# Attention, Fourier mixing and an MLP on one core: the same steps in another written order

## The chip, the cores and the metric

The kernel runs on one core of a Trainium2 chip. A core has five engines with an instruction queue each: TensorE (PE, matrix products), VectorE (DVE), ScalarE (ACT), GpSimd (POOL) and SyncE (SP, which here only issues DMAs). An engine runs its queue strictly in order; across engines, semaphores make an instruction wait for its inputs and for the release of a buffer. 16 DMA engines move data between HBM and the on-chip memory (SBUF); PE writes its products to a second memory (PSUM). The metric is the device time of one execution in microseconds, here the median of several runs. Lower is better.

## The reference

The inputs are q, k and v of shape 4 x 8 x 768 x 64 (batch, heads, sequence, head width) and the two weights of an MLP, 512 x 2048 and 2048 x 512, all float32.

```python
# attention over selected blocks of 64 keys
k_rep = k.reshape(B, H, n_blocks, block, D).mean(axis=3)
gate_scores = np.einsum('bhsd,bhnd->bhsn', q, k_rep)
gate_scores = np.where(causal, gate_scores, -1000000000.0)
top_idx = np.argsort(gate_scores, axis=-1)[..., -top_k:]          # top_k = 3
# mask: the selected blocks and the own block, causal inside
scores = np.where(mask, scale * np.matmul(q, k.transpose(0, 1, 3, 2)), -1000000000.0)
attn = softmax(scores); x = np.matmul(attn, v)                    # then heads side by side: 4 x 768 x 512
# Fourier mixing, normalisation, MLP
mixed = np.real(np.fft.fft(np.fft.fft(x, axis=1), axis=2))
u = x + mixed
un = (u - mean(u)) / np.sqrt(var(u) + 1e-06)
out = u + np.maximum(un @ w_ch1, 0.0) @ w_ch2
```

## The kernel before

**Tiling.** The attention works on 16 pairs of heads, P = 0 to 15; pairs 4b to 4b+3 make up batch b. When the four pairs of a batch are done, its x (768 x 512) is folded, goes through two Fourier transforms as matrix products, is normalised, and goes through the MLP. So the work of a batch is a long chain of small steps (attention, Fourier) and then a block of pure PE work (the MLP), and the attention of later pairs is interleaved with the MLP of earlier batches.

**The order.** No planner runs in the kernel. The string `ORDER` (from line 112) lists 1011 steps, each a name and its numbers. Lines 753 to 758 call the function behind each (the table `WORK`, line 735) in that order, inside `tc.manual_schedule` for all five engines. Each engine's queue is therefore the list of the steps that issue on it, in the order of the string; where two steps on different engines stand in the string relative to each other means nothing by itself. Semaphores and the choice of a free buffer are the framework's.

**The steps, by engine.**

- SP: `Lk:P`, `Lq:P`, `Lv:P` load k, q and v of a pair (line 264; k and q as two DMAs of 192 KB, v as one of 384 KB; three buffers each for k and q, two for v). `LF`, `LT`, `Lc`, `Li` load constants; `LF` and `LT` are the Fourier matrices. `un:b,i` for b of 1 and more is a pair of transposing DMAs (line 593). `od:b,i` writes a block of the result.
- POOL: `W:c` and `X:c` issue the DMAs of the MLP weights, `W:0` 512 KB, `W:1` and `W:2` 768 KB, `X:0` and `X:1` 1024 KB as fp16 in SBUF (lines 721 to 729); their targets are tiles of their own, so they wait for nothing but their turn in POOL's queue. `qs:P` and `vc:P` cast q and v, `d:P,i` clears the upper triangle of a diagonal block (line 437), `K:P` copies the mask rows, `nr:b` makes the reciprocal root, `pg:b` is a tiny copy that waits for the folded tile of batch b.
- PE: `tk:P` and `tq:P` transpose k and q (line 292), `g:P` gives the gate scores, `s:P,i` six tiles of scores (lines 409 to 421, from pair 7 on line 414), `v:P` the product with v (line 449), `y` and `m` the Fourier products, `xt` three transposes of batch 0, `w:b,i` 16 steps of the first MLP product (lines 629 and 631) and `c:b,i,h` 12 half-steps of the second (line 656; line 648 for the last block).
- DVE: `ks`, `kh`, `qc` on the transposed k and q, `gt`, `gx`, `gl`, `gm` the choice of blocks, `x:P` the softmax division, `fs`, `fd`, `f` the folds, `tr` a reversed copy, `u` the sum x + mixed, `un:0,i` copies of batch 0, `bn` and `nv` the statistics, `r:b,i` the relu of every fourth `w`, `o` the last sum.
- ACT: `kc:P` casts the transposed k, `e:P,i` the exponentials (line 431), `ty` a copy, `xu` the centred u, and the other `r`.

**Waits around the change.** `tk:P` needs `Lk:P`, `tq:P` needs `Lq:P`. `v:P` needs `vc:P`, which needs `Lv:P`, and all of `d:P,i`. `s:P,i` needs `qs:P`, `kc:P` and `gm:P` (from pair 7 on also `K:P`). `e:P,i` needs `s:P,i`. `f:b,*` and then `y:b,*` need `x` of the batch's four pairs. `w:b,i` needs all `un` of the batch. All PSUM tiles share four buffers. u has five buffers of two blocks each, which `od` releases.

Of the kernel before, what the change touches and what calls it, by code (L numbers as in the profile page):

```python
# [787 lines left out]
```

## Time and profile before

| what | us |
|---|---|
| median of 3 runs | 297.64 |
| lowest and highest of them | 297.6, 297.93 |
| profiled execution, first to last instruction | 295.6 |
| PE busy in it | 286.5 |
| DVE busy | 192.5 |
| ACT busy | 164.2 |
| POOL busy | 111.1 |

The table's last rows are the busy time of each engine inside the span. PE is busy for most of it, but the profile models the ends of matmuls, so a matmul that is held up counts as busy. A row of 40 digits gives the busy share of 40 equal slices in tenths. Queue q0 carries the weights, which POOL issues; q1 carries what SP issues. For a DMA the profile has the start of its issue and the time to its landing. In a list of stages the numbers are the length, the busy time and the count of instructions of PE, PE's weight loads, DVE, ACT and POOL, the granted clock of PE, the share of the DMA engines and GB/s.

### The profile page before, as it was taken

The page shows a single profiled execution, that of the slowest core. Times are in us where ns is not written, and L with a number is a line of the kernel's source. Part 1 is how long each engine was busy: PE and PEld are TensorE (multiplying, and loading weights), DVE is VectorE, ACT ScalarE, POOL GpSimd, SP SyncE. Part 2 cuts the span into 40 slices and gives each one's busy share as a digit, 9 for nine tenths or more (in the row PEclk, how much of TensorE's full clock was granted, in tenths as well). Part 3 has the DMA queues.
Part 4 walks back from the last instruction along what each step waited for, and adds up shares of the span by engine and source line. Part 5 has one row for each costly group of instructions (what it writes and reads, how often), then busy time and mean ns, then how long its engine had stood idle before and what let it go on. Part 6 is the DMA issues. An engine that isn't in the chain of part 4 may idle for free.

```text
span 295.6 us, 6738 instructions
## 1 busy us (share of the span) xinstructions
PE 286.5 (97%) x2633; PEld 180.2 (61%) x2633; DVE 192.5 (65%) x597; ACT 164.2 (56%) x205; POOL 111.1 (38%) x286
## 2 busy tenths in 40 slices
PE   8899999999999999999999999999999999999995
PEld 4566767765676556656757667446666554555453
DVE  2999999986988638987796577714493282700132
ACT  3698989749578841677788843165524250155000
POOL 2267528528776289064753363220303000110000
PEclk9999999999999999999999999999999999999999
DMA  8999999997999727477000005311000052300023
GB/s 197 268 228 230 262 245 199 195 230 118 226 185 211 168 55 186 118 164 176 3 0 2 0 9 136 38 72 71 2 1 2 32 103 44 142 0 2 0 91 125
DMA packets 93200, 33.53 MB, mean 113 GB/s; under 512 B 85936, under 2 KB 89968, under 8 KB 93168
## 3 DMA queue, kind: packets, MB, share of 16 engines
q1 hardware_dynamic: 87504, 28.47, 40.6%
q0 software_dynamic: 3664, 4.19, 9.1%
q10 hardware_dynamic: 2000, 0.44, 0.7%
q8 instruction: 21, 0.34, 0.5%
q14 instruction: 11, 0.09, 0.1%
HBM read 28.63 MB, written 6.29 MB: 118 GB/s over the span
## 4 chain that ended last, share of the span: by engine, by line
PE 84%; DVE 7%; ACT 6%; DMA 1%; issue 1%; DVEq 0%; ACTq 0%
PE c L656 26%; PE h L629 19%; PE h L631 10%; PE sc L414 7%; PE av L449 6%; ACT pt L431 5%; PE tp L292 5%; PE yp L519 2%; PE mx L552 2%; DVE q L316 2%; PE mx L553 1%; PE warmps L693 1%; DVE u L566 1%; PE g L342 1%; PE c L648 1%; PE sc L409 1%
## 5 line engine op out<-in xcount | busy, mean ns | idle before, releaser
L431 ACT ACTIVATE pt<-sc 128x1024 f16<-128x1024 f32 (+1 forms) x96 | 83.3, 923 | 26.6 <-PE sc L414 19.7
L629 PE MATMUL h<-unT,w 128*128 128x512 f16 x256 | 85.1, 379 | 0.0
L656 PE MATMUL c<-w_sb,hT 128*128 128x512 f16 x368 | 83.8, 379 | 0.0
L631 PE MATMUL h<-unT,w 128*128 128x256 f16 x256 | 69.7, 272 | 0.4 <-DMA unT<-x 0.4
L641 ACT ACTIVATE hT<-h 128x768 f16<-128x768 f32 x48 | 37.8, 813 | 43.7 <-PE h L631 43.7
L656 PEld LDWEIGHTS <-hT 128*128 128x128 f16 x368 | 35.6, 98 | 39.3 <-issue 0.5
L437 POOL TENSOR_SCALAR_AFFINE_SELECT pt<-pt 128x256 f16<-128x256 f16 x96 | 37.5, 414 | 58.5 <-ACT pt L431 57.6
L629 PEld LDWEIGHTS <-w 128*128 128x128 f16 x256 | 25.0, 97 | 29.2 <-issue 1.3
L668 DVE SCALAR_TENSOR_TENSOR u<-c,rs,u 128x512 f32<-128x512 f32 (+1 forms) x25 | 17.5, 725 | 31.2 <-PE c L656 30.4
L639 DVE TENSOR_SCALAR hT<-h 128x768 f16<-128x768 f32 x16 | 15.3, 955 | 29.7 <-PE h L631 29.6
L578 ACT ACTIVATE x<-u,nm 128x512 f16<-128x512 f32 x24 | 15.9, 715 | 22.5 <-DVE nm L572 22.3
L292 PE MATMUL tp<-id,nat 128*128 128x128 f32 x192 | 27.5, 284 | 0.6 <-ACT pt L431 0.3
L631 PEld LDWEIGHTS <-w 128*128 128x128 f16 x256 | 25.0, 98 | 4.3
L225 POOL TENSOR_SCALAR_AFFINE_SELECT qk<-mt 32x160 f16<-32x160 f16 x72 | 23.1, 341 | 10.8 <-DVE mt L386 9.1
L414 PE MATMUL sc<-qk 96*128 96x512 f16 (+3 forms) x144 | 26.8, 305 | 0.0
L225 POOL TENSOR_SCALAR_AFFINE_SELECT qk<-q 64x768 f16<-64x768 f32 (+1 forms) x25 | 20.6, 825 | 14.8 <-DVE q L316 14.1
L292 PEld LDWEIGHTS tp<-id,nat 128*128 128x128 f32 x192 | 22.2, 146 | 5.7 <-issue 1.6
L449 PE MATMUL av<-v,pt 128*128 128x65 f16 x672 | 23.0, 193 | 0.1
L449 PEld LDWEIGHTS <-pt 128*128 128x128 f16 x672 | 22.0, 97 | 1.7 <-POOL pt L437 0.5
L297 DVE TENSOR_REDUCE kr<-tp 128x12 f32<-128x768 f32 x16 | 15.1, 945 | 5.9 <-PE tp L292 5.9
L222 POOL TENSOR_TENSOR t<-vr,rs 128x6 f32<-128x6 f32 x12 | 2.4, 199 | 43.5 <-DVE rs L609 42.9
L414 PEld LDWEIGHTS <-qk 96*128 96x128 f16 x144 | 13.3, 97 | 8.9 <-issue 0.5
(95 smaller groups left out, 351.2 us busy)
## 6 DMA issues: line engine op xcount, KB each, us to landing
nat<-in_v_dram SPq DMA_DIRECT2D x16, 384.0 KB, 4.7
nat<-in_k_dram SPq DMA_DIRECT2D x31, 192.0 KB, 3.5
nat<-in_q_dram SPq DMA_DIRECT2D x31, 192.0 KB, 3.9
out_dram<-u SPq DMA_DIRECT2D x23, 256.0 KB, 2.1
w_sb<-in_moe_w_ch_dram POOLq DMA_DIRECT2D x2, 1024.0 KB, 10.2
w<-in_moe_w_ch_dram POOLq DMA_DIRECT2D x2, 768.0 KB, 8.4
fs_sb<-c_FS SPq DMA_DIRECT2D x1, 582.0 KB, 5.1
w<-in_moe_w_ch_dram POOLq DMA_DIRECT2D x1, 512.0 KB, 7.3
```

The source lines that it names most:

```text
L225: nc.gpsimd.affine_select(out=out, in_=in_, pattern=[[0, i] for i in n], base=0, channel_multiplier=0, compare_op=ALU.is_ge, fill=0.0)
L292: nc.tensor.transpose(ps[:, 128 * st:128 * st + 128], src[:, st, :], id32)
L414: nc.tensor.matmul(ps[:, e, co:co + q1 - q0], qk[0:96, e, 1, 128 * jt:128 * jt + 128], qk[0:96, e, 0, q0:q1], start=True, stop=True)
L431: nc.scalar.activation(out=d["pt"][:, o:o + 2 * n].rearrange("p (e c) -> p e c", e=2), in_=d["sc", i][:, :, 0:n], func=AF.Exp, scale=0.125)
L437: nc.gpsimd.affine_select(out=dg, in_=dg, pattern=[[0, 2], [1, 128]], base=0, channel_multiplier=-1, compare_op=ALU.is_ge, fill=0.0)
L449: nc.tensor.matmul(av[:, e, 66 * st:66 * st + 65], pt[:, co:co + 128], vv[:, e, jt, 0:65], start=(cnt == 0), stop=(cnt == 20))
L578: nc.scalar.activation(out=x_b[:, 2 * kp + k2, :], in_=u_b[:, k2, :], func=AF.Identity, scale=0.0625, bias=nm[:, k2:k2 + 1])
L629: nc.tensor.matmul(hp[:, 0:512], w1s, unT[:, dt, 0:512], start=(dt == 0), stop=(dt == NDT - 1))
L631: nc.tensor.matmul(hp[:, 512:768], w1s, unT[:, dt, 512:768], start=(dt == 0), stop=(dt == NDT - 1))
L641: nc.scalar.activation(out=hT, in_=hp, func=AF.Relu)
L656: nc.tensor.matmul(c_ps[b, g[0]][:, st - g[0], :], h_t[b, it][:, 128 * st:128 * (st + 1)], w2_sb[:, it, :], start=(it == 0), stop=(it == N ...
L668: nc.vector.scalar_tensor_tensor(out=o, in0=ps, scalar=st_t[b][1][:, st:st + 1], in1=o, op0=ALU.mult, op1=ALU.add)
```

## The change

Only the string `ORDER` changes. It holds the same 1011 steps, each once, in another order on all five engines. On POOL, the weight loads `W:1`, `X:1`, `X:0` and `W:2` move to the front part of the queue, `W:0` moves behind `vc:5`. On SP, among others, `Lv:2` and `Lv:3` move ahead of `Lv:1`, and `Lk:7`, `LF`, `Lk:8` and `LT` change places with other loads. On PE, DVE and ACT neighbouring steps change places in the attention part (`v:1` now stands ahead of `s:3,1`, for one), and around each MLP the mix of `c`, `w`, `s` and `v` steps is another. In the new string the steps of POOL and SP stand in bunches; the sequence on each engine is what counts.

```diff
 ORDER = """
-Lk:1 Lq:1 Lk:2 Lq:2 tk:0 ks:0 tq:0 Lq:3 Lk:3 kh:0 qc:0 iz:1 tk:1 qs:0 kc:0 g:0 ks:1 iz:0 gt:0 tq:1
-kc:1 gx:0 Lq:4 Lv:0 Lk:4 Lv:1 kh:1 gl:0,0 tk:2 gl:0,1 gm:0 kc:2 qc:1 s:0,3 s:0,2 ks:2 e:0,3 qs:1
-tq:2 Lq:5 Lk:5 s:0,5 qc:2 g:1 e:0,5 e:0,2 kh:2 s:0,4 gt:1 qs:2 s:0,0 e:0,4 gx:1 s:0,1 d:0,2 tq:3
-gl:1,0 e:0,0 gl:1,1 tk:3 gm:1 e:0,1 d:0,0 qc:3 g:2 d:0,3 kc:3 d:0,5 s:1,5 gt:2 d:0,4 s:1,0 e:1,5
-qs:3 ks:3 s:1,4 e:1,0 tq:4 d:0,1 gx:2 vc:0 e:1,4 s:1,3 qc:4 s:1,1 Lv:2 e:1,3 s:1,2 gl:2,0 kh:3
-tk:4 gl:2,1 e:1,2 d:1,3 gm:2 g:3 d:1,4 ks:4 d:1,0 v:0 d:1,5 gt:3 vc:1 kc:4 gx:3 e:1,1 s:2,5 Lv:3
-Lq:6 LF:0 Lq:7 Lk:6 Lk:7 LT:0 s:2,3 kh:4 gl:3,0 e:2,5 gl:3,1 s:2,4 e:2,3 d:1,1 x:0 tq:5 qs:4 e:2,4
-g:4 d:2,3 gm:3 qc:5 s:2,0 d:2,4 s:2,2 d:1,2 e:2,0 gt:4 d:2,5 tk:5 vc:2 gx:4 e:2,2 s:2,1 ks:5 d:2,0
-Lv:4 Lq:8 Lk:8 s:3,1 e:2,1 v:1 gl:4,0 kh:5 gl:4,1 kc:5 d:2,1 gm:4 d:2,2 s:3,2 x:1 e:3,1 vc:3 g:5
-e:3,2 Lv:5 Lc:0 d:3,1 s:3,5 gt:5 s:3,0 fs:0,1 e:3,5 s:3,3 d:3,2 gx:5 e:3,0 s:3,4 fs:1,1 tq:6
-gl:5,0 e:3,3 fs:0,0 v:2 gl:5,1 fs:1,0 e:3,4 d:3,3 qc:6 d:3,0 s:4,5 x:2 d:3,4 s:4,4 e:4,5 d:3,5
-s:4,0 qs:5 v:3 e:4,0 gm:5 fs:2,0 fs:2,1 e:4,4 s:5,5 x:3 s:4,1 e:5,5 s:5,1 e:4,1 fd:2,0 s:4,2 s:5,0
-fs:3,1 e:5,1 fs:3,0 s:5,2 fd:2,1 e:5,0 fd:3,1 s:4,3 fd:3,0 e:5,2 tk:6 f:0,1 f:0,2 e:4,3 Lk:9 Lq:9
-tk:7 f:0,3 e:4,2 f:0,0 y:0,1 ks:7 pg:0 W:0 kc:6 y:0,0 tr:0,1 d:4,0 kc:7 d:4,4 d:4,5 ks:6 d:5,5
-d:4,1 ty:0,1 tr:0,0 s:5,3 d:5,2 s:5,4 d:4,3 kh:6 W:1 ty:0,0 m:0,2 qs:6 e:5,3 u:0,2 m:0,1 vc:4
-e:5,4 m:0,0 u:0,1 xu:0,2 d:5,4 tk:8 d:5,1 d:4,2 u:0,0 xu:0,1 d:5,0 xt:0,2 W:2 g:6 un:0,2 xu:0,0
-xt:0,1 gt:6 tq:8 un:0,1 kc:8 xt:0,0 qc:8 tq:7 un:0,0 qs:8 v:4 Lq:10 Lk:10 Lv:6 Lq:11 qc:7 bn:0,3
-w:0,4 d:5,3 qs:7 bn:0,1 w:0,5 r:0,4 gx:6 ks:8 w:0,6 r:0,5 gl:6,0 kh:7 gl:6,1 x:4 w:0,7 r:0,6 gm:6
-w:0,3 r:0,7 s:6,5 r:0,3 s:6,1 e:6,5 s:6,3 e:6,1 kh:8 s:6,2 fs:4,0 bn:0,4 w:0,2 e:6,2 d:6,1 X:0
...
-vc:7 e:7,2 tq:10 gl:8,1 Lv:9 r:0,1 X:1 gm:8 s:7,4 qc:10 w:0,15 d:7,2 e:7,4 K:8 bn:0,0 g:9 r:0,15
...
-m:1,0 o:0,0 m:1,1 od:0,0 o:0,1 d:9,2 od:0,1 v:8 u:1,1 m:1,2 u:1,0 xu:1,1 c:0,4,0 gl:11,0 xu:1,0
...
-qc:13 vc:13 bn:1,4 s:11,2 d:10,5 x:9 s:11,4 vc:12 e:11,2 c:0,5,1 bn:1,1 Lv:14 Lv:15 e:11,4 s:11,0
-o:0,5 s:11,5 w:1,11 e:11,5 od:0,5 o:0,4 e:11,0 kh:12 bn:1,5 od:0,4 s:11,3 w:1,7 e:11,3 r:1,11
...
-d:14,5 x:12 qs:15 s:14,3 m:2,2 e:14,3 bn:2,0 c:1,4,0 x:13 fs:13,0 g:15 fs:13,1 c:1,5,0 u:2,2
-fs:12,0 xu:2,2 gt:15 c:1,2,0 bn:2,4 un:2,2 gx:15 c:1,5,1 gl:15,0 fs:12,1 gl:15,1 gm:15 bn:2,5
-c:1,4,1 K:15 c:1,2,1 o:1,4 od:1,4 o:1,5 s:14,1 od:1,5 s:15,4 e:14,1 s:15,0 c:1,3,0 e:15,4 d:14,1
-d:14,3 e:15,0 d:15,4 s:14,4 s:14,2 d:15,0 e:14,4 s:15,2 c:1,3,1 e:15,2 e:14,2 s:15,3 o:1,3 w:2,1
...
-c:2,1,0 r:2,12 ty:3,0 c:2,0,1 c:2,1,1 m:3,0 o:2,0 c:2,2,0 od:2,0 u:3,0 o:2,1 xu:3,0 m:3,1 od:2,1
-c:2,4,0 u:3,1 un:3,0 xu:3,1 bn:3,2 m:3,2 c:2,3,0 u:3,2 un:3,1 bn:3,3 xu:3,2 c:2,5,0 bn:3,0 un:3,2
-bn:3,5 c:2,3,1 bn:3,1 c:2,4,1 c:2,2,1 w:3,3 c:2,5,1 r:3,3 o:2,3 w:3,7 od:2,3 o:2,4 o:2,2 od:2,4
...
-r:3,12 r:3,9 r:3,14 c:3,0,0 w:3,15 c:3,4,0 r:3,15 c:3,1,0 c:3,0,1 c:3,1,1 c:3,5,0 o:3,0 od:3,0
-o:3,1 c:3,3,0 od:3,1 o:3,5 od:3,5 c:3,4,1 c:3,2,1 o:3,4 od:3,4 c:3,3,1 c:3,5,1 o:3,3 od:3,3 o:3,2
-od:3,2 o:3,6 od:3,6
+Lk:1 Lq:1 Lk:2 Lq:2 tk:0 Lk:3 Lq:3 ks:0 kc:0 tq:0 tk:1 kh:0 qc:0 g:0 tq:1 tk:2 kc:1 iz:0 iz:1 ks:1
+kc:2 gt:0 W:1 qs:0 Lq:4 Lv:0 Lk:4 Lv:2 Lq:5 Lv:3 Lk:5 Lv:1 Lk:7 Lq:6 kh:1 gx:0 gl:0,0 gl:0,1 gm:0
+s:0,3 tq:2 s:0,2 s:0,5 e:0,3 qc:1 e:0,5 g:1 e:0,2 s:0,4 e:0,4 s:0,0 e:0,0 ks:2 s:0,1 qc:2 e:0,1 tq:3
+gt:1 gx:1 gl:1,0 kh:2 gl:1,1 X:1 d:0,5 d:0,2 qs:1 gm:1 qc:3 tk:3 g:2 s:1,5 kc:3 e:1,5 s:1,0 s:1,4
+e:1,0 tq:4 gt:2 s:1,3 ks:3 s:1,1 gx:2 kh:3 s:1,2 tk:4 qc:4 g:3 e:1,4 gl:2,0 gl:2,1 gm:2 qs:2 d:0,1
+d:0,0 vc:0 d:0,4 d:0,3 X:0 d:1,5 vc:2 W:2 d:1,4 ks:4 v:0 s:2,5 s:2,3 s:2,4 gt:3 e:1,3 e:1,2 gx:3 x:0
+tq:5 kh:4 g:4 e:1,1 kc:4 e:2,5 e:2,3 e:2,4 fs:0,1 gl:3,0 s:2,0 qc:5 gl:3,1 gt:4 s:2,2 e:2,0 s:2,1
+gm:3 gx:4 fs:0,0 d:1,2 qs:3 d:1,1 qs:4 d:2,3 d:1,3 d:1,0 vc:1 tk:5 ks:5 e:2,1 v:1 gl:4,0 kh:5 x:1
+kc:5 s:3,1 e:2,2 e:3,1 s:3,2 e:3,2 g:5 gl:4,1 fs:1,0 s:3,5 e:3,5 s:3,4 s:3,0 s:3,3 e:3,4 tq:6 e:3,0
+gt:5 e:3,3 LF:0 Lk:8 LT:0 Lv:5 Lv:4 Lk:6 Lv:6 Lq:11 Lk:10 Lv:7 Lk:12 Lq:8 Lq:7 Lv:8 Lk:9 Lq:9 Lc:0
+d:2,2 d:2,5 d:2,4 d:3,1 vc:3 d:2,0 d:3,5 d:2,1 d:3,2 d:3,0 d:3,3 d:3,4 qs:5 gm:4 gx:5 gl:5,0 fs:1,1
+gl:5,1 qc:6 v:2 s:4,5 e:4,5 s:4,0 s:4,4 v:3 gm:5 s:5,5 e:4,0 s:4,1 e:4,4 e:5,5 x:2 e:4,1 s:5,0 e:5,0
+s:5,2 e:5,2 s:4,2 s:5,1 s:4,3 tk:7 e:4,2 fs:2,0 fs:2,1 fd:2,1 x:3 fd:2,0 fs:3,0 fs:3,1 fd:3,0 fd:3,1
+f:0,2 f:0,3 f:0,0 f:0,1 y:0,1 tr:0,1 e:4,3 e:5,1 ks:7 ty:0,1 y:0,0 tr:0,0 s:5,3 kc:7 tk:6 m:0,2 ks:6
+s:5,4 ty:0,0 kc:6 e:5,3 m:0,1 kh:6 u:0,2 e:5,4 m:0,0 g:6 u:0,1 u:0,0 xu:0,2 xu:0,1 vc:5 W:0 d:5,5
+d:4,1 qs:6 vc:4 d:5,2 pg:0 d:5,3 d:4,0 d:4,5 d:5,4 d:4,3 d:5,1 vc:6 d:4,2 d:5,0 d:4,4 xu:0,0 xt:0,2
+tk:8 gt:6 un:0,2 xt:0,1 un:0,1 tq:8 xt:0,0 un:0,0 kc:8 gx:6 qc:8 v:4 w:0,4 w:0,6 w:0,5 tq:7 ks:8
...
+bn:1,3 u:1,0 s:10,1 xu:1,0 e:10,1 m:1,2 u:1,2 c:0,5,0 xu:1,2 od:0,1 od:0,2 od:0,3 un:1,0 un:1,1
+un:1,2 tq:13 v:9 qc:13 e:11,5 s:10,2 e:10,2 c:0,5,1 s:10,5 s:10,4 e:10,5 tq:12 s:11,2 s:11,4 e:10,4
+tk:13 tk:12 w:1,6 x:9 o:0,4 w:1,14 e:11,4 w:1,11 e:11,2 w:1,7 kc:12 o:0,5 kc:13 fs:8,1 qc:12 s:11,3
...
+c:1,2,0 g:15 o:1,1 c:1,3,0 s:14,0 m:2,2 gt:15 c:1,5,1 gx:15 gl:15,0 gl:15,1 gm:15 d:14,2 K:15 s:15,0
+e:14,0 xu:2,0 s:15,5 u:2,2 c:1,3,1 o:1,5 s:14,5 e:15,5 e:15,0 xu:2,2 s:15,3 e:15,3 s:15,4 o:1,4
+o:1,3 bn:2,4 c:1,2,1 e:15,4 s:15,1 s:15,2 e:14,5 od:1,0 Lv:14 od:1,1 un:2,1 un:2,0 un:2,2 s:14,1
+w:2,13 e:15,1 w:2,5 w:2,4 e:15,2 e:14,1 r:2,5 r:2,4 o:1,2 bn:2,5 bn:2,2 nv:2 d:15,3 d:14,0 d:15,5
...
+r:2,9 w:2,15 r:2,10 r:2,15 ty:3,0 c:2,0,1 o:2,0 y:3,1 c:2,1,1 ty:3,1 tr:3,0 m:3,0 c:2,2,1 tr:3,1
+m:3,1 c:2,4,0 o:2,1 m:3,2 u:3,0 c:2,4,1 c:2,5,0 u:3,1 u:3,2 bn:3,2 c:2,3,1 c:2,5,1 od:1,3 od:1,4
+od:1,2 od:2,0 od:2,1 od:1,5 xu:3,0 xu:3,1 xu:3,2 un:3,0 un:3,1 un:3,2 bn:3,3 w:3,11 bn:3,0 o:2,5
...
+c:3,3,0 c:3,3,1 c:3,0,1 o:3,3 o:3,4 c:3,1,0 o:3,0 c:3,1,1 c:3,2,1 o:3,1 o:3,2 c:3,5,1 od:3,5 od:2,5
+od:3,3 od:2,4 od:2,3 od:2,2 od:3,4 od:3,1 od:3,0 od:3,2 o:3,6 od:3,6
 """
```

## The prediction

> **What bounds the kernel now.** I read the page first, then sums by stage, the chain of waits, the DMA issues in order of time, and the landing times of single loads. Columns are named where they are not plain.
>
> The page: busy time by engine, then the span in 40 slices of 7.4 us, then two DMA queues with packets, MB and share of the span.
>
> ```profile
> PE 286.5 (97%) x2633; PEld 180.2 (61%) x2633; DVE 192.5 (65%) x597; ACT 164.2 (56%) x205; POOL 111.1 (38%) x286
> ...
> DMA  8999999997999727477000005311000052300023
> ...
> q1 hardware_dynamic: 87504, 28.47, 40.6%
> q0 software_dynamic: 3664, 4.19, 9.1%
> ```
>
> PE looks full, but the 97% hides a start that is not. The stages (length, then busy us of each engine, clock, DMA share, GB/s) show it:
>
> ```profile
> 0.00:20.00 20.00, 17.24 (x151) 10.87 (x152) 14.03 (x51) 12.28 (x16) 7.13 (x28) 1.00 1.01 227
> 20.00:32.00 12.00, 11.56 (x214) 8.30 (x214) 11.36 (x51) 10.48 (x13) 7.94 (x17) 1.00 1.08 249
> 32.00:58.60 26.60, 24.51 (x388) 19.07 (x385) 25.38 (x70) 24.43 (x31) 13.59 (x28) 1.00 1.06 220
> 58.60:292.20 233.60, 233.16 (x1890) 141.93 (x1886) 141.31 (x429) 117.06 (x146) 82.40 (x217) 1.00 0.37 84
> ```
>
> From 58.6 us, where the first `w:0,4` (line 629) starts, PE idles 0.44 us in 233.6. Before that ACT and DVE are nearly full while PE's matmuls are stretched. And in the first three stages the DMA engines are at a share of 1.01 to 1.08: full. The chain of waits (start, us) agrees: ACT and DVE carry it until the first batch's `un` copies, PE after that.
>
> ```profile
> 32.02 1.95 ACT pt L431 x2
> ...
> 39.94 5.89 ACT pt L431 x7
> ...
> 54.52 0.60 DVE unT L590
> ...
> 58.76 0.22 PE h L629
> ```
>
> How far ahead of their use do the q, k and v loads run? In the order of time, SP's and POOL's issues:
>
> ```profile
> 6.32 1.29 SPq L275 DMA_DIRECT2D nat<-in_k_dram  x2
> ...
> 22.28 2.79 SPq L270 DMA_DIRECT2D nat<-in_v_dram  x2
> ```
>
> ```profile
> 45.55 0.95 POOL L723 DMA_DIRECT2D w<-in_moe_w_ch_dram  x1
> ...
> 49.04 0.77 POOL L723 DMA_DIRECT2D w<-in_moe_w_ch_dram  x1
> ...
> 53.39 0.76 POOL L723 DMA_DIRECT2D w<-in_moe_w_ch_dram  x1
> ```
>
> The first row is `Lk:2`; issue to landing is 2.9/3.5/5.0 us (min, median, max) for the q and k loads of 2 to 20 us, so its second half, issued at 6.90, lands about 10.3. Its transposes `tk:2` start at 10.4: almost no lead. The last of the three POOL rows (`W:2`) and two q halves issued at 56.1 and 56.5, beside it, show what a weight does to a load. The landing lines, first `W:2`, then those two:
>
> ```profile
> DMA to landing us min/median/max: 8.6/8.6/8.6
> ```
>
> ```profile
> DMA to landing us min/median/max: 6.4/6.8/7.2
> ```
>
> The loads take 6.4 and 7.2 us where the quiet median is 3.5, and land at 62.5 and 63.7, just after the weight (53.4 + 8.6 = 62.0). A weight in flight holds the loads back until it has landed.
>
> **The change, part by part.** Every step is kept. I sorted both orders by engine.
>
> *Weights, POOL queue.* Before: `W:0 W:1 W:2` follow `pg:0` (45.4 us), `X:0` and `X:1` come at 67.5 and 79.7, when only the loads of later pairs are left. After: `W:1` is POOL's first step after the constants' memsets, which end at 2.4 us; `X:1` follows `qs:0`, `X:0` follows `vc:0` and two `d`, `W:2` follows `vc:2`. Only `W:0` stays late. So four of five weights, 768+1024+1024+768 KB, are put beside loads that have no lead. The price of one: `W:0`, `W:1`, `W:2` land at 45.55+7.3 = 52.9, 49.04+8.2 = 57.2 and 62.0, back to back, thus 4.4 and 4.7 us for 768 KB, mean 4.55; by size 6.1 for 1024 KB. Four: 2x4.55 + 2x6.1 = 21.3 us of held loads. Queue 0's busy share gives a check: 9.1% of 295.6 is 26.9 us for 4.19 MB, so 23.5 for these 3.67 MB. Lower bound: a weight only costs the extra latency seen above, 6.5 - 3.5 = 3 us, so 12 us. I take 21.3, because the loads beside `W:2` landed after it.
>
> Rules of the Trainium skill pull both ways here. Its page "DMA: Bandwidth & Descriptors", section "Rules for kernel authors", says to issue a DMA early and wait for it late, which by itself speaks for this change and would price the move at nothing. The same page, "Issuing engines are not separate DMA queues", says that DMAs of all issuing engines run on the same 16 engines and interleave, which speaks against it; the 6.4 to 7.2 us landings agree with that one. By the page's ceiling of 435 GB/s the 3.67 MB would be an estimated 8.4 us, and the sum below would end 12.9 us lower.
>
> *Loads, SP queue.* `Lv:2` and `Lv:3` are moved ahead of `Lv:1`, which is now the 16th load of 384 KB. Before, the 16th is `Lv:3`, issued at 24.70, landed 4.1 later: 28.8, with 1.9 us in it in which SP waited for a buffer (the row at 22.28 lasts 2.79, its two issues 0.9). Without that wait 26.9; with the weights 26.9 + 21.3 = 48.2. All four are issued ahead of that: `W:2` needs `vc:2`, whose load stands three loads earlier.
>
> *What queues behind it.* In the new PE order `v:1` stands ahead of `s:3,1` and of all scores of pairs 3 to 5 (before, `s:3,1` went first), and `x:1` stands ahead of `gm:4` on DVE. So the late `Lv:1` stops PE, then ACT, then DVE. `vc:1` 0.9 and its start 0.1: 49.2; `v:1` 1.45 (line 449): 50.7; `s:3,1` 0.6: `e:3,1` at 51.3. Before it starts at 32.0: **+19.3**. ACT and DVE idle meanwhile, but their queues are fixed and nothing of pairs 3 to 5 can be pulled ahead.
>
> *From `e:3,1` to `w:0,4`.* Before: 26.6 us, with ACT 24.4 and DVE 25.4 busy, so it can't shrink by more than 1.2. ACT has the same steps there. DVE has `gl:4,1`, `gm:4` and one `fs` more behind `x:1` (0.2+0.5+0.35): **+1.0**. `w:0,4` starts at 51.3+27.6 = 78.9. Hidden, with their cover: `LT` lands about 8 us after `Lv:1` (five loads), 56.5, while `y:0,1` comes at 45+20 = 65; `W:0`, behind `vc:5` now, is issued about 59 and lands at 66, while its first user `w:0,3` comes after 79; `Lq:8` waits behind `Lk:12` for `tk:6` to free a buffer, some 6 us ahead of `tq:8`, bounds 0 to 1, taken 0.
>
> *After 78.9.* The same PE work, plus `tq:7` (0.66), which moved behind `w:0,5`. The start of each MLP needs the last `u`, `xu` and transposes; before, `m:3,2` ends at 240.2 and the last transpose lands at 247.3: 7.1 us. Cover by `c` steps (1.73 each) behind the last `m` shrinks: batch 1 from 4 to 2, but with 5.7 us of other steps beside; batch 2 from 8 to 3 (5.2 + 2.8 of scores = 8.0, less the two `e` of 1.3 now ahead of the last `xu`); batch 3 from 5 to 4 (6.9 against 7.1). I take 0 + 0.6 + 0.2, **+1.5** with `tq:7`; bounds -0.4 (all of PE's idle time there goes) and +5 (each transition falls short by a whole `c`). Moving `X:0` and `X:1` away from 67 to 90 us takes away 3.8 us of POOL's waiting for v loads; PE did not wait, so nothing. The end is the same: `c:3,5,1`, `o:3,6` (0.48), `od:3,6`; the batch 2 outputs now issued in the last stretch take 0.33 each on SP under seven `c` steps.
>
> Sum: 19.3 + 1.0 + 1.5 = 21.8 on a span of 295.6: 317.4. The median of the runs is 297.64, 2.04 above that span; with it 319.4.
>
> **The rivals.**
> *Only half the weights hit.* `X:0` and `W:2` start late enough that `Lk:5` and `Lv:1` slip past them, and only `W:1` and `X:1` count: 4.55+6.1 = 10.65, `Lv:1` at 37.6, `e:3,1` 3.1 later at 40.7, which is +8.7; with 1.0 and 1.5 that is +11.2, 308.8. For it: `X:0` waits for `vc:0`, and the loads have run on until then. Against: `W:2` needs `vc:2`, whose load is only three loads of about 1.5 us ahead of `Lv:1`, and `X:0` is then still in flight.
> *The transitions break.* The load delay as forecast, and each shortened cover falls short by about a `c` plus the output wait that frees a `u` buffer (five buffers; `u:2,2` now waits for `od:1,1`, about 2.1 us to land): 319.4 + 3x3 = 328. For it: three covers shrink together. Against: 7.1 us against 6.9 and 8.0 is a near fit.
> *Not slower.* The load stream has spare rate that the weights use, so `Lv:1` lands before its use. For it: the DMA rate is 227 GB/s in the first stage and 249 in the second, so it isn't everywhere at its highest. It decides if the four weights cost the loads under 1.5 us in all instead of 21.3 (`Lq:2`, issued until 9.2, lands at 11.6 and `tq:2` starts at 13.1; the k loads have 0.1). Then 297.6 with at most 0.4 of idle to gain and 1.5 to lose: 297.2 to 299.1. Against: the 6.4 to 7.2 us landings.
>
> **How the numbers follow.** As forecast, 312 to 325: 0.66. Half the weights, 304 to 312: 0.14. Transitions break, above 325: 0.10. Not slower or hardly: 0.06 faster (an idle part of the start filled better than I see), 0.02 within 0.2%, which is about what a measurement of this kernel can tell from no change, 0.02 a few us slower. So slower 0.92, same 0.02, faster 0.06. The range leaves out the extremes: 305 to 326.
>
> **What would show it.** Right: in the stages before about 79 us ACT and DVE lose some 20 us of busy share, POOL's `vc` and PE's transposes wait for `nat` loads, a v:1 (line 449) starts near 49, the first line 629 near 79; the DMA row stays at 9 through the start and falls to low digits earlier relative to the MLP; from line 629 on PE is as full as before. Wrong: the loads keep their 3.5 us landing beside `W:1` and `X:1`, or PE gets work in the gap, which its order does not allow by my reading; or the loss sits at the batch transitions instead.

## The result, and the profile after

The changed kernel takes 329.61 us (median of four runs, 328.33 to 329.81) against 297.62 us for the kernel before: 1.107 times as long, 95% interval 1.1042 to 1.1097. The forecast was 319.4 us with a range of 305 to 326. The direction was right; the size was 10.2 us short and outside the range. The profiled execution took 328.33 us, the fastest of the four, with a span of 326.4, 30.8 us more than the 295.6 before. In the changed kernel's profile all lines of code have numbers lower by two, because the new string is two lines shorter.

The page first: busy time by engine, then the DMA share and PE's granted clock in 40 slices of 8.2 us, then the two DMA queues and the bytes read from HBM.

```profile
PE 292.9 (90%) x2633; PEld 183.3 (56%) x2633; DVE 198.6 (61%) x597; ACT 164.9 (51%) x205; POOL 113.9 (35%) x286
...
PEclk9759976999999999999999999999999999999999
DMA  9999999899407900022891000051400016100143
...
q1 hardware_dynamic: 87504, 28.47, 36.7%
q0 software_dynamic: 3664, 4.19, 7.6%
...
HBM read 28.63 MB, written 6.29 MB: 107 GB/s over the span
```

The bytes are those of before. The queue rows count a weight as it lands, in fp16. In HBM the weights are float32, twice as many bytes: q, k and v make 18.87 MB, and only with 8.39 MB for the weights do the inputs come near the 28.63 read. The DMA row stays near 9 for the first ten slices: the weights have moved to the start. The clock row is new: PE is at half its clock for parts of the first 55 us. By stages (length, busy us of PE, its weight loads, DVE, ACT and POOL, clock, DMA share, GB/s):

```profile
0.00:20.00 20.00, 8.91 (x42) 5.01 (x43) 7.39 (x30) 4.54 (x6) 4.24 (x20) 0.86 1.10 209
20.00:32.00 12.00, 11.28 (x126) 7.77 (x127) 8.28 (x30) 8.53 (x11) 5.46 (x10) 0.81 1.07 241
32.00:58.60 26.60, 17.91 (x300) 12.67 (x294) 16.76 (x63) 14.98 (x18) 11.24 (x23) 0.81 1.11 224
```

In the first 20 us PE now has 42 instructions where it had 151, and ACT 6 where it had 16. The DMA engines are as full as before, so the weights found no idle time in them. What they carry is seen in three windows: without a weight in flight (20 to 30 us), with `X:0` and `W:2` in flight (35 to 43 us), and with `X:1` and the end of `W:1` (10 to 18 us); a row is a queue with its packets, MB and share of the 16 engines:

```profile
q1 hardware_dynamic: 9559, 2.40, 107.0%
```

```profile
q0 software_dynamic: 1147, 1.25, 95.6%
q1 hardware_dynamic: 809, 0.20, 19.5%
```

```profile
q0 software_dynamic: 1026, 1.07, 78.8%
q1 hardware_dynamic: 2739, 0.69, 43.7%
```

The loads' queue brings 2.40 MB in 10 us in the first window, 0.20 MB in 8 us in the second and 0.69 MB in 8 us in the third: 240 GB/s against 25 and 86. So beside weights the loads move at a tenth to a third of their rate. In the second window the weights' 1.25 MB are some 2.5 MB read, so an estimate of what the engines read there is 2.7 MB in 8 us, 338 GB/s: more than without weights, but little of it for the loads. The Trainium skill bears on that: its page "DMA: Bandwidth & Descriptors", section "Queues, rings and completion order", says that a DMA engine takes turns between the queues that have work, one packet at a time. The 1147 weight packets beside 809 load packets of the second window are near that, the 1026 beside 2739 of the third are not, and whether a packet of the profile is a packet of the page no run shows. A weight packet here is 1.25 MB / 1147 = 1.1 KB and a load packet 0.25 KB, so even equal turns would be far from equal bytes.

The chain of waits of the changed kernel (start, us, what) shows who stands on the critical path of the start:

```profile
8.42 11.26 DMA nat<-in_k_dram
...
33.43 15.08 DMA nat<-in_v_dram
48.52 0.06 issue
48.57 0.92 POOL v L223
49.49 0.04 issue
49.54 2.47 PE av L447 x42
```

The second half of `Lk:2` takes 11.26 us to land, `Lv:1` 15.08. PE's waits up to 82 us (us in total, times, longest) name the same two kinds of load:

```profile
PE tp L290 <- DMA nat<-in_k_dram: 13.2, 3, 4.9
PE av L447 <- POOL v L223: 3.8, 1, 3.8
PE yp L517 <- DVE fg L499: 1.9, 1, 1.9
```

Behind the start, PE is not as full as it was. First the stage from `w:0,4` to the last product before, then the same stage after, each with its own ends:

```profile
58.60:292.20 233.60, 233.16 (x1890) 141.93 (x1886) 141.31 (x429) 117.06 (x146) 82.40 (x217) 1.00 0.37 84
```

```profile
81.76:323.05 241.29, 235.72 (x1896) 142.98 (x1892) 143.91 (x423) 117.41 (x146) 81.95 (x213) 1.00 0.26 66
```

It is 7.7 us longer, and PE idles 5.57 us in it where it idled 0.44. Seven places of the changed kernel make up 4.92 of them; each row is a PE instruction with the idle time before it and who released it:

```profile
130.34 0.48 PE L340 MATMUL g<-q,krb 128*32 128x160 f32 x8 [0.55 <-ACT qk L309]
...
141.53 0.27 PE L550 MATMUL mx<-fd_sb,ty 128*128 128x256 f16 x1 [0.70 <-ACT pt L429]
...
162.58 0.38 PE L627 MATMUL h<-unT,w 128*128 128x512 f16 x1 [0.48 <-DVE kr L295]
...
185.13 0.38 PE L627 MATMUL h<-unT,w 128*128 128x512 f16 x1 [0.88 <-ACT pt L429]
...
200.24 0.92 PE L447 MATMUL av<-v,pt 128*128 128x65 f16 x25 [0.96 <-DVE tr L536]
...
205.05 0.27 PE L550 MATMUL mx<-fd_sb,ty 128*128 128x256 f16 x1 [0.51 <-DVE kr L295]
...
317.61 0.59 PE L654 MATMUL c<-w_sb,hT 128*128 128x512 f16 x2 [0.84 <-DVE u L666]
```

In none of the seven is the releaser what the waiting product reads (a `w` step reads no `pt` and no `kr`). The reading is that ACT or DVE had to finish with an earlier product first, since all products share four PSUM buffers. The trace fits it: `g:11`, `m:1,1`, `w:1,11`, `w:1,3` and `m:2,0` each start 0.05 us behind the end of a step that reads one of the last few products ahead of them (`kc:11`, `e:9,4`, `ks:12`, `e:13,0`, `ks:15`), and `v:12` 0.15 us behind `tr:2,0`. The last row, `c:3,1,1` behind `o:3,0`, is of another kind (experiment 8). None of the seven is the first `w` step of a batch.

When some steps start, in us of the two profiled executions:

| step | before | forecast | after |
|---|---|---|---|
| `Lv:1` landed | 22.1 | 48.2 | 48.5 |
| `v:1` | 30.5 | 49.2 | 49.5 |
| `e:3,1` | 32.0 | 51.3 | 53.0 |
| `w:0,4` | 58.6 | 78.9 | 81.8 |
| `c:3,5,1` | 290.2 | 312.0 (290.2 + 21.8) | 321.1 |

The 30.8 us of span are 21.0 up to `e:3,1` (forecast 19.3), 2.1 from there to `w:0,4` (forecast 1.0) and 7.7 behind it (forecast 1.5).

### The profile page after: what moved, and what is told of

Same layout as the page of the kernel before. It is cut to its first block, busy times and chain, and to the rows that moved or that the text cites. A ratio compares the mean times of both kernels' runs of the same rounds, so it can differ in the third digit from the quotient of the medians.

```text
span 326.4 us, 6729 instructions
## 1 busy us (share of the span) xinstructions
PE 292.9 (90%) x2633; PEld 183.3 (56%) x2633; DVE 198.6 (61%) x597; ACT 164.9 (51%) x205; POOL 113.9 (35%) x286
## 3 DMA queue, kind: packets, MB, share of 16 engines
q0 software_dynamic: 3664, 4.19, 7.6%
HBM read 28.63 MB, written 6.29 MB: 107 GB/s over the span
## 4 chain that ended last, share of the span: by engine, by line
PE 65%; DMA 9%; ACT 9%; DVE 9%; POOL 5%; issue 1%; SPq 1%; ACTq 0%; POOLq 0%
PE c L654 23%; PE h L627 14%; PE h L629 7%; PE av L447 5%; PE sc L412 5%; DMA nat<-in_v_dram 5%; ACT pt L429 4%; DMA nat<-in_k_dram 3%; PE tp L290 3%; POOL qk L223 3%; ACT qk L309 2%; PE yp L517 2%; ACT ty L530 1%; DMA nat<-in_q_dram 1%; PE mx L550 1%; DVE sd L220 1%
## 5 line engine op out<-in xcount | busy, mean ns | idle before, releaser
L435 POOL TENSOR_SCALAR_AFFINE_SELECT pt<-pt 128x256 f16<-128x256 f16 x96 | 38.6, 426 | 78.4 <-ACT pt L429 77.6
L290 PE MATMUL tp<-id,nat 128*128 128x128 f32 x192 | 29.3, 295 | 14.2 <-DMA nat<-in_k_dram 13.2
L290 PEld LDWEIGHTS tp<-id,nat 128*128 128x128 f32 x192 | 23.1, 150 | 19.2 <-issue 13.9
L447 PE MATMUL av<-v,pt 128*128 128x65 f16 x672 | 24.2, 196 | 4.8 <-POOL v L223 3.8
L447 PEld LDWEIGHTS <-pt 128*128 128x128 f16 x672 | 23.2, 100 | 7.2 <-issue 4.6
L220 POOL TENSOR_TENSOR t<-vr,rs 128x6 f32<-128x6 f32 x12 | 2.7, 225 | 51.3 <-DVE rs L607 50.7
L564 DVE SCALAR_TENSOR_TENSOR u<-mx,x 128x512 f32<-128x512 f32 x24 | 15.6, 688 | 6.7 <-PE mx L551 6.7
```

The source lines that it names most:

```text
L290: nc.tensor.transpose(ps[:, 128 * st:128 * st + 128], src[:, st, :], id32)
L435: nc.gpsimd.affine_select(out=dg, in_=dg, pattern=[[0, 2], [1, 128]], base=0, channel_multiplier=-1, compare_op=ALU.is_ge, fill=0.0)
L447: nc.tensor.matmul(av[:, e, 66 * st:66 * st + 65], pt[:, co:co + 128], vv[:, e, jt, 0:65], start=(cnt == 0), stop=(cnt == 20))
```

## The experiments

The questions were: is it the weights or the rest of the order; which loads gate the start; what are the 7.7 us at the end; and does the halved clock cost anything. Times are medians, ratios are to the kernel before, with their 95% interval. "Loss behind `w:0,4`" is worked out from a trace: for all neighbouring PE steps behind `w:0,4`, the time from start to start less what such a step takes where nothing holds it, summed; 3.3 us before, 10.3 after. (10.3 less 3.3, and 0.66 for `tq:7`, which the change moved into this stretch, make the 7.7 us above.) In the kernels of the experiments lines are lower by another two (exp is L427).

**1. The new order with the weights late again.**

```diff
-... kc:2 gt:0 W:1 qs:0 ... X:1 d:0,5 ... vc:0 d:0,4 d:0,3 X:0 d:1,5 vc:2 W:2 ... vc:5 W:0
+... kc:2 gt:0 qs:0 ... d:0,5 ... vc:0 d:0,4 d:0,3 d:1,5 vc:2 ... vc:5 W:1 ... d:4,1 W:0 ... d:4,4 W:2 ... d:6,1 X:0 ... vc:7 X:1
```

> The new order, with only the five weight loads moved in POOL's queue to about where they stood before (W:1 behind vc:5, W:0 behind d:4,1, W:2 behind d:4,4, X:0 behind d:6,1, X:1 behind vc:7). Theory 'weights hold the loads': the first w:0,4 falls back from 81.8 us to 59-62 us, and what is left of the loss is the 7.0 us that PE loses behind w:0,4 plus tq:7's 0.7: time 304 to 308 us. Rival 'the other reordering costs the start' (v:1 ahead of s:3,1, the new order of the loads): w:0,4 stays at 75 us or later and the time at 322 us or more.

Measured 319.28 us, 1.0713 [1.0691, 1.0736]. `w:0,4` came at 63.4 instead of 81.8, so 18.4 of the 23.2 us there were the weights'. But the time gave back only 10.3, and the expectation missed: behind `w:0,4` PE lost 19.9 us, 7.07 of them in one place between `v:7` and `s:8,4`. The timeline of POOL, then of PE:

```profile
99.05 0.90 POOL L221 TENSOR_SCALAR_AFFINE_SELECT v<-nat 128x768 f16<-128x768 f32 x1 [9.40 <-DMA nat<-in_v_dram]
```

```profile
100.73 1.89 PE L445 MATMUL av<-v,pt 128*128 128x65 f16 x31 [6.15 <-POOL pt L433]
```

POOL stood 9.4 us for `Lv:9`, which was issued at 91.7 with `X:1` (83.4 to some 96) in flight. I had put `X:1` back, but in the new order other loads stand beside that place.

**2. The old order with four weights early.** The counterpart: only `W:1 X:1 X:0 W:2` take their new places.

```diff
-qs:0 kc:0 ... vc:0 e:1,4 ... vc:2 gx:4 ... kh:6 W:1 ty:0,0 ... xt:0,2 W:2 g:6 ... d:6,1 X:0 e:6,3 ... r:0,1 X:1 gm:8
+W:1 qs:0 X:1 kc:0 ... vc:0 X:0 e:1,4 ... vc:2 W:2 gx:4 ... kh:6 ty:0,0 ... xt:0,2 g:6 ... d:6,1 e:6,3 ... r:0,1 gm:8
```

> The order of before, with only W:1, X:1, X:0 and W:2 moved to the places of the new order in POOL's queue (first; behind qs:0; behind vc:0; behind vc:2). Theory 'weights hold the loads': w:0,4 at 74 to 82 us instead of 58.6, time 313 to 321 us. Rival 'the other reordering costs the start': w:0,4 stays within 3 us of 58.6 and the time within 3 us of 297.6.

Measured 314.81 us, 1.0574 [1.0556, 1.0592]: the time is as expected, and the rival is out. The weights' early places alone cost 17.2 us. The profiled execution was this kernel's fastest (310.89): there `tk:2` came 9.6 us later than before, `e:3,1` 10.1, `w:0,4` 13.3 (at 71.9, 2 us ahead of the expected range) and the end 13.5, with 3.5 us of loss behind `w:0,4`. So in this execution early weights delay the start and nothing else; where the slower ones lose up to 4.7 us more was not traced.

**3 and 4. Splices.** For each engine, the steps written ahead of `w:0,4` in one order, then the rest as the other has it.

```diff
-ORDER = the new string
+ORDER = steps of the old string ahead of w:0,4, then the others as the new string has them   (3)
+ORDER = steps of the new string ahead of w:0,4, then the others as the old string has them   (4)
```

> Each engine follows the old order for all steps that stand ahead of w:0,4 in the old string, and the new order for the rest. Theory 'the new order loses PE time of its own behind w:0,4': 297.6 + 7.0 + 0.7 = 305 us, range 303 to 307. Rival 'the loss behind w:0,4 is an echo of the late loads of the start': 297 to 300 us.

> Each engine follows the new order for all steps that stand ahead of w:0,4 in the new string, and the old order for the rest. If the start's loss (23.2 us at w:0,4) and the rest's loss simply add: 297.6 + 23.2 = 321 us, range 319 to 323. If the old rest is hurt by the late start as well: 326 us or more; if it catches up some of it: under 318 us.

The new start with the old rest took 322.25 us, 1.0808 [1.0792, 1.0824], as expected: `w:0,4` 24.3 us late, and only 3.3 us of loss behind it, as before. What the changed kernel loses on top, 329.6 - 322.3 = 7.4 us, belongs to the new rest. The old start with the new rest missed: 322.38 us, 1.0824 [1.0796, 1.0852], where about 305 was expected. `w:0,4` came on time (58.57), but PE then stood 15.6 us. The waits between 56 and 92 us:

```profile
POOL v L221 <- DMA nat<-in_v_dram: 20.3, 2, 16.2
...
PE sc L410 <- POOL qk L221: 15.4, 1, 15.4
```

The splice itself had put `X:1` and `X:0` (58.9 and 59.8 us) in front of `Lv:8`, and in the new POOL order `vc:8` stands ahead of `K:7`, for which `s:7,5` waits. So this splice does not measure the new rest alone; it shows the same mechanism a third time.

**5. PE kept warm.** 68 products of 128x512 on zeros, whose result nobody uses, stand in the four long waits of the start (added work, nothing left out).

```diff
+    def warm(i, n):
+        zps = pst([128, 512], f"warm{i}")
+        for _ in range(n):
+            nc.tensor.matmul(zps, wsrc[:, 0:128], wsrc, start=True, stop=True)
-... tk:1 ... tk:2 ... tk:5 ks:5 e:2,1 v:1
+... z:0,18 tk:1 ... z:1,20 tk:2 ... z:2,14 tk:5 ks:5 e:2,1 z:3,16 v:1
```

> The new order, with 68 filler matmuls (128x512 on zeros, results not used) put on PE where it waits for loads: 18 ahead of tk:1, 20 ahead of tk:2, 14 ahead of tk:5, 16 ahead of v:1, at 0.22 us each less than the waits of 3.6 to 5.0 us. Theory 'the idle waits halve PE's granted clock, and that is the 1.7 to 2.8 us by which the start was worse than forecast': the clock stays at 1.0, v:1 takes 1.45 us instead of 2.47, w:0,4 starts at 79 to 80 us instead of 81.8, time 326.5 to 328 us. Rival 'the clock costs nothing since the loads set the pace': w:0,4 within 0.5 us of 81.8, time 329 to 330.5 us.

Measured 329.6 us, 1.1091 [1.1026, 1.1157] (328.33 to 332.82): the median did not move. The profiled execution is the slowest of the four. Its first three stages, then `v:1` there and in the changed kernel (nanoseconds of one product, min/median/max):

```profile
0.00:20.00 20.00, 16.41 (x79) 8.36 (x79) 7.38 (x30) 4.54 (x6) 4.24 (x20) 1.00 1.09 207
20.00:32.00 12.00, 10.42 (x142) 7.18 (x142) 9.45 (x33) 9.80 (x12) 6.33 (x12) 1.00 1.03 233
32.00:58.60 26.60, 20.26 (x230) 11.59 (x232) 12.23 (x43) 9.90 (x13) 7.37 (x15) 0.87 1.05 213
```

```profile
L445 PE MATMUL av<-v,pt x42: 191/193/197, 55.2 to 56.5; 128*128 128x65 f16 x42
```

```profile
L447 PE MATMUL av<-v,pt x42: 216/243/247, 49.5 to 51.8; 128*128 128x65 f16 x42
```

The clock stayed full through the first two stages and `v:1` took 1.45 us instead of 2.47. Yet the start was not sooner: `tq:5` came 1.5 us earlier, but `tk:5` then waited for `Lk:5`, which landed at 48.0 instead of 44.5. And the last fillers ran past their gap, as the rows of `vc:1` and of those fillers show:

```profile
49.49 0.91 POOL L221 TENSOR_SCALAR_AFFINE_SELECT v<-nat 128x768 f16<-128x768 f32 x1 [11.61 <-DMA nat<-in_v_dram]
```

```profile
49.47 5.93 PE L734 MATMUL warm<-zeros 128*128 128x512 f16 x16
```

`v:1` could have started at 50.4 and started at 55.2; `w:0,4` came at 86.4, in neither range of the expectation. So the run prices the fillers together with the clock, and what the half clock alone costs stays open; only the 1.0 us at `v:1` and the 0.4 at `s:3,1` can be read off. The Trainium skill's page "TensorE: Matmul & The Clock Gate", section "HAM oscillation — how this bites in real kernels", tells authors to leave no idle gaps over about 3.4 us on PE. The changed kernel's clock does halve in and after its gaps of 3.4 to 4.9 us, so the mechanism agrees; whether filling the gaps without such an overrun is worth time, no run here shows.

**6. Two weights later.** In the new order, `X:0` and `W:2` move behind `vc:1`, and so behind `Lv:1`.

```diff
-vc:0 d:0,4 d:0,3 X:0 d:1,5 vc:2 W:2 d:1,4 ... d:1,0 vc:1 tk:5
+vc:0 d:0,4 d:0,3 d:1,5 vc:2 d:1,4 ... d:1,0 vc:1 X:0 W:2 tk:5
```

> The new order, with only X:0 and W:2 moved behind vc:1 in POOL's queue, so that Lk:5 and Lv:1 run ahead of them. Theory 'each weight holds exactly the loads that are in flight or issued behind it': e:3,1 falls from 53.0 to 42-45 us (W:1 and X:1 alone), w:0,4 from 81.8 to 71-76 us, time 319 to 324 us. Rival 'the total of DMA work ahead of w:0,4 counts, wherever it stands': w:0,4 within 2 us of 81.8, time 327 us or more.

Measured 324.99 us, 1.0925 [1.0887, 1.0963]: 4.6 us less, 1 us short of the theory's range. `e:3,1` came at 44.8, 8.2 us sooner than in the changed kernel, but `w:0,4` only 2.1 sooner, at 79.6 instead of 71 to 76. PE's longest wait between 56 and 80 us says what took over:

```profile
PE tp L288 <- DMA nat<-in_q_dram: 6.0, 1, 6.0
```

That is `tq:8`, waiting for `Lq:8`. Three quarters of the gain went into the next late load.

**7. `Lv:1` at its old place in the SP queue**, with `vc:1` and `vc:2` exchanged and `v:1` behind `s:3,1` as before.

```diff
-Lv:0 Lk:4 Lv:2 Lq:5 Lv:3 Lk:5 Lv:1 ... v:1 gl:4,0 kh:5 x:1 kc:5 s:3,1
+Lv:0 Lk:4 Lv:1 Lv:2 Lq:5 Lv:3 Lk:5 ... gl:4,0 kh:5 kc:5 s:3,1 v:1 x:1
```

> The new order with Lv:1 back behind Lk:4, vc:1 and vc:2 exchanged on POOL and Lv:1's users v:1 and x:1 behind s:3,1; the weights stay in front. Theory 'v:1's new place adds to the weights' delay': v:1 waits no more, but tk:5 still does (Lk:5 lands behind the weights at 44.5), so e:3,1 starts at 46 to 49 us instead of 53.0, w:0,4 at 76 to 79 instead of 81.8, time 324 to 327 us. Rival 'v:1's place is of no account, the next late load takes over at once': w:0,4 within 1 us of 81.8, time 328.5 us or more.

Measured 328.78 us, 1.1035 [1.0996, 1.1075]: 0.8 us at most, and the rival held. Now `tq:5` waits between 30 and 60 us:

```profile
PE tp L288 <- DMA nat<-in_q_dram: 7.3, 1, 7.3
```

So `Lv:1`, on which the whole forecast was built, was the load that happened to be last. With it put ahead, `Lq:5` and `Lk:5` stand one load later in the same queue; that the bytes ahead of the loads set the pace, whichever load is last, is the reading that fits experiments 2, 6 and 7.

**8. `o:3,0` written behind `c:3,1,1`.** No engine's own sequence changes; only the place of a DVE step beside a PE step in the string.

```diff
-c:3,1,0 o:3,0 c:3,1,1
+c:3,1,0 c:3,1,1 o:3,0
```

> The new order with o:3,0 written behind c:3,1,1 instead of ahead of it. No engine's queue changes; only the direction of the dependency between the two (both use the PSUM tile of blocks 0 and 1) does. Theory 'some of the late loss is PE waiting for readers of PSUM tiles': the 1.0 us between c:3,1,0 and c:3,1,1 goes, time 328.4 to 329.0 us. Rival 'the place in the string between two engines means nothing': no change, 329.3 to 330 us.

Measured 327.96 us (326.86 to 328.73), 1.1017 [1.0977, 1.1058]; the interval overlaps that of the changed kernel, so the time alone does not decide. The trace does: the 1.00 us between `c:3,1,0` and `c:3,1,1` is gone, and the loss behind `w:0,4` is 9.1 instead of 10.3. So the sentence in the section on the kernel before, that the place of steps on different engines relative to each other means nothing by itself, is not right. Blocks 0 and 1 of the second MLP product share one PSUM tile: `o:3,0` reads the first block and `c:3,1,1` writes the second. Written behind the reader, the product waits for it, though it touches other data. So this place is a shared tile, not a buffer that is taken over, and the run shows nothing of the other places.

**9 and 10. The next late loads.** Number 9 is number 6 with `Lk:6` and `Lq:8` moved ahead on SP's queue; number 10 moves `W:0` later as well.

```diff
-LF:0 Lk:8 LT:0 Lv:5 Lv:4 Lk:6 Lv:6 Lq:11 Lk:10 Lv:7 Lk:12 Lq:8 Lq:7
+LF:0 Lk:8 Lk:6 Lq:8 LT:0 Lv:5 Lv:4 Lv:6 Lq:11 Lk:10 Lv:7 Lk:12 Lq:7      (9 and 10)
-vc:5 W:0 d:5,5 ... d:4,4
+vc:5 d:5,5 ... d:4,4 W:0                                                  (10)
```

> The changed order with X:0 and W:2 behind vc:1, as in the run with two weights later, and now Lk:6 and Lq:8 also put ahead on SP's queue, right behind Lk:8 (in the changed order Lq:8 stands behind Lv:5, Lv:4, Lv:6, Lq:11, Lk:10, Lv:7 and Lk:12). Theory, the late Lq:8 held w:0,4 at 79.6 us in that run (PE stood 6.0 us before tq:8 for a q load): tq:8 has its data in time, that wait is gone, w:0,4 starts between 72.4 and 75 (e:3,1 at 44.8 plus 27.6 to 30), the time falls from 325.0 by 4 to 7 us, to 318 to 321. Rival, the sum of all loads and weights sets the pace whatever their order, or W:0 at 60 us holds another load that is needed as much: w:0,4 stays at 78 or later and the time at 323 or more.

> As the run with Lk:6 and Lq:8 ahead, and W:0 also moved later on POOL's queue, from behind vc:5 to behind d:4,4, some 10 us. Theory, the loads that w:0,4 needs are in by then: no further gain of more than 1 us against that run, or a loss where r:0 or the first w:0 step that reads W:0 waits for it. Rival, W:0 in flight holds what the loads of 60 to 70 us bring: a further 2 to 4.5 us (its own duration beside nothing is 4.55) earlier, 314 to 318.

Number 9 took 322.34 us, 1.0828 [1.0804, 1.0852], between theory and rival: the wait of `tq:8` is gone and `w:0,4` is at 75.8, 3.8 us sooner, but now PE waits for `LT`, which the two loads had been put ahead of:

```profile
PE yp L515 <- DMA fs_sb<-c_FS: 3.4, 1, 3.4
```

Number 10 took 323.57 us, 1.0873 [1.0844, 1.0903]: no further gain, as the theory had it.

**11. Number 1 with `X:1` behind `vc:9`** instead of `vc:7`.

```diff
-vc:7 X:1 d:6,3 ... d:6,4 vc:9
+vc:7 d:6,3 ... d:6,4 vc:9 X:1
```

> The changed order with the weights put back late, as in the first experiment (319.3 us), but X:1 behind vc:9 instead of behind vc:7. Theory: the 7.07 us for which PE stood between v:7 and s:8,4 were Lv:9 held by X:1; they go, and the 1.1 us behind w:0,2 with them or not, so 311 to 313.5. Rival, X:1 only shared the guilt and the order of loads itself is late there (Lv:9 stands behind four q and k loads): at least 3 us of that stall stay, 315 or more.

Measured 310.89 us, 1.0438 [1.0416, 1.0459]. The 7.07 us are gone: they were `X:1`'s. This is the new order with the weights late (`W:1` and `W:0` go out at 41.7 and 43.7 us, the first of the kernel before at 45.6), and it costs 13.3 us: `e:3,1` 2.2 us later than before, `w:0,4` 4.5, the end 13.4, with 11.6 us of loss behind `w:0,4`. The places of loss listed for the changed kernel stand here too, and in experiments 1, 3, 6 and 9, each within 0.02 us of the same size whatever the start does. In the stage from 32 to 58.6 us PE waits for no load; its longest wait there is 2.6 us for the folds on DVE, which the new order bunches just ahead of `y:0,1`:

```profile
32.00:58.60 26.60, 20.84 (x336) 15.55 (x333) 24.47 (x61) 22.13 (x28) 13.85 (x29) 1.00 1.03 221
```

```profile
PE yp L515 <- DVE fg L497: 2.6, 1, 2.6
```

**12. A version that could beat both.** The kernel before with `Lk:15` and `Lq:15` behind `un:1,2` on SP's queue, since PE waits there for a transposed `un:1`. SP's steps:

```diff
-un:1,1 un:1,0 Lk:15 Lq:15 un:1,2 Lv:14
+un:1,1 un:1,0 un:1,2 Lk:15 Lq:15 Lv:14
```

> The kernel before with one edit: Lk:15 and Lq:15 stand behind un:1,2 on SP's queue instead of ahead of it. Before, PE waits about 0.5 us between w:1,11 and s:11,3 for a transposed un:1 that SP issues behind these two loads. Theory: that wait goes, 297.1 +- 0.2, the only version here that could beat both kernels. Rival: the next thing in the queue is late by as much, or PE's idling moves on: 297.4 to 297.9.

Measured 297.03 us, 0.9983 [0.9971, 0.9996]. The 0.54 us between `w:1,11` and `s:11,3` is gone from the trace. It is the fastest kernel of this study, by a gain at the edge of what can be measured.

**13. Three of the late places mended at once.** Number 8's edit, `s:13,0` behind `w:1,3`, and `c:0,3,1` with `o:0,3` behind `s:9,0`.

```diff
-o:0,1 c:0,3,1 y:1,1 s:9,4 ty:1,1 o:0,3 e:9,4 s:10,0 s:9,0 e:9,0
+o:0,1 y:1,1 s:9,4 ty:1,1 e:9,4 s:10,0 s:9,0 c:0,3,1 o:0,3 e:9,0
...
-s:13,0 w:1,13 w:1,3 qc:15
+w:1,13 w:1,3 s:13,0 qc:15
```

> The changed order with three local moves behind w:0,4 and nothing else: o:3,0 written behind c:3,1,1 (as in the run before, worth 1.0 us), s:13,0 moved behind w:1,3 on PE (PE stands 1.04 us between w:1,13 and w:1,3 for an exp of ACT), and c:0,3,1 with o:0,3 moved behind s:9,0 (PE stands 0.86 us between s:9,0 and m:1,1, also for an exp). Theory, the 7 us lost behind w:0,4 are places at which PE's next product stands too close behind the one whose buffer it takes over: each place can be mended alone, the losses there fall from 2.9 to under 0.5 and the time to 326.5 to 327.3. Rival, the waits only move to the next product: the loss behind w:0,4 stays at 9 us or more and the time at 328 or more.

Measured 332.38 us, 1.1171 [1.1136, 1.1206]: 2.8 us slower than the changed kernel, so the rival held and the theory fell. The three stalls are gone from their places, but new ones stand next to the two moved products, and the loss behind `w:0,4` is 12.6 us:

```profile
140.48 1.24 PE L410 MATMUL sc<-qk 96*128 96x512 f16 x4 [1.14 <-DVE tr L534]
...
146.26 0.28 PE L548 MATMUL mx<-fd_sb,tr 128*128 128x256 f16 x1 [1.11 <-DVE tr L534]
...
191.26 0.38 PE L625 MATMUL h<-unT,w 128*128 128x512 f16 x1 [1.11 <-ACT pt L427]
```

In the second row the product waits for what it reads, the reversed copy. The third shows a wait that moved with its cause: in the changed kernel `w:1,3` started 0.05 us behind `e:13,0`, which reads `s:13,0`; with `s:13,0` moved, `w:1,2` does. That moving one long product shifts the distance between every product and the reader it waits for is the reading that fits.

## Why the forecast was wrong in size

**What the change costs, taken apart.** Two kernels with one half of the change each nearly add up to the whole: early weights in the old order +17.2 us (314.8), the new order with late weights +13.3 us (310.9), together 328.1 against 329.6 measured. The forecast had 21.3 for the weights, and for everything else 21.8 - 21.3 = 0.5. In the changed order, too, the weights come to 329.6 - 310.9 = 18.7. So the weights were sized 2.6 to 4.1 us too high, and the order itself 12.8 too low. Of the 10.2 us by which the sum fell short, 9.0 are in the profiled span: 1.7 up to `e:3,1`, 1.1 to `w:0,4` and 6.2 behind it; the rest is the median, which lies 1.3 above the profiled execution.

**Weights beside loads without lead: right, and the landing luckier than it looks.** `Lv:1` landed at 48.5 where 48.2 was forecast; all four weights were in front of it. But in experiment 11, with no weight ahead, it landed at 28.7, where the forecast had 26.9. So the weights held it by 19.8 us instead of 21.3, and two errors of 1.5 and 1.8 us cancel. The rival in which only half of them hit was excluded by that landing, the rival "not slower" by the second experiment: 17.2 us against the 1.5 up to which it held. By the Trainium skill's page "DMA: Bandwidth & Descriptors", the rule to issue a DMA early (section "Rules for kernel authors") would have priced the move at nothing, and the ceiling of 435 GB/s (section "Specifications") at an estimated 8.4 us; the runs say 17 to 19. That estimate counted the bytes that land; with the float32 bytes that are read it is 16.9 us.

**`Lv:1` as the gate: right in the number, wrong as a cause.** With it put back (7) another load stood in its place; with two of the four weights moved behind it (6, 9) `e:3,1` gained 8 us, and the following loads took back all but 2.1 and 5.9 of it at `w:0,4`. I followed one load through the queue, where the whole queue is late.

**From `e:3,1` to `w:0,4`, +1.0: mis-sized, 2.1.** `e:3,1` was itself 1.7 us later than forecast, 1.4 of that because `v:1` and `s:3,1` ran at half clock (2.47 us instead of 1.45, 0.98 instead of 0.58). By experiment 11 the start of the new order costs 4.5 us even without early weights; 2.2 of it are there by `e:3,1`, for which the forecast's steps gave 2 us of gain. The 1.9 us for which PE waits for the folds in front of `y:0,1` (2.6 in experiment 11) were not in the sum at all: I had counted DVE's added steps (0.2+0.5+0.35) and not the place of the folds among them. The forecast's reading that ACT and DVE are nearly full before `w:0,4` does not hold for the first 20 us either, in which they were busy 12.3 and 14.0.

**After `w:0,4`, +1.5: the step that failed.** It measured 7.7, and by experiments 4 and 11 it is the new rest's own, 7.4 and 9.0 us, whatever the start does. I looked for the loss at the transitions between batches, where the cover of `c` steps shrinks. There is none at the first `w` step of any batch. The loss lies inside the batches, where, as read from the trace, a product takes over a PSUM buffer whose reader on ACT or DVE is late. The forecast names the four buffers nowhere in its sum: it costed moved PE steps by their duration and took PE's order as free. The rival "the transitions break" has nearly the measured time (328), but by a mechanism that did not occur, and the forecast's sign to look for, PE as full as before from line 629 on, failed.

**What stays open.** That a late reader in PSUM sets a late wait is shown by a run for one place (8), and there it is a tile that two blocks share. For the others, where a buffer is taken over, it is read from the trace: the product starts right behind a reader of an earlier one, and in experiment 13 one such wait moved with its reader. That attempt to mend two of them made the kernel slower. How much of the 7.7 us is a matter of each single place, and how much of the whole sequence, was not settled; nor were the cost of the half clock, and the 1.5 us by which the two halves of the change fall short of the whole.

## What to carry to other kernels

Before moving a large transfer to an earlier place, list what is in flight beside it and how much lead each of those has; a transfer with nothing waiting for it can still cost its full time to those that do. When one late load is found, ask which is next: mending it is worth only the distance to the second-latest. And when steps change places on the engine that is the bound, check for each the buffer that it takes over and who must have read it by then; a sequence can be slower with every step unchanged and every input on time.

## What the runs showed of the hardware

- Weights issued by POOL leave the loads of SP a tenth to a third of their rate: 0.20 MB in 8 us beside 1.25 MB of weights and 0.69 MB in 8 us beside 1.07 MB, against 2.40 MB in 10 us alone (changed kernel).
- A weight that is turned from float32 into fp16 on its way counts in the queue rows as it lands, half of what is read: 4.19 MB in the queue, while the 28.63 MB read from HBM are only reached with 8.39 MB for the weights.
- PE's clock was at half in parts of the first 55 us, in and after gaps of 3.4 to 4.9 us; a `v` step took 2.47 us instead of 1.45. Fillers kept it full through the first 32 us and the median time did not change, but the last of them held `v:1` back by 4.8 us.
- Some versions spread more than others: the old order with early weights ran from 310.89 to 315.55 us, where the kernel before stayed within 296.74 and 298.66 beside all experiments. Early weights alone do not explain it, for the new start with the old rest (number 4) stayed within 321.76 and 322.61.
